# Paired routing counts, a first expert fed by columns, gathers in a row, and half tiles interleaved with whole ones

## The chip, the cores and the metric

The kernel runs on one core of a Trainium2 chip. The metric is the device time of one execution in microseconds (us); of several runs the median is taken. The engines are PE (TensorE, the matmuls), DVE (VectorE), ACT (ScalarE), POOL (GpSimd) and SP (SyncE, which here only issues DMAs). Below, a matmul written `128*64 128x256` holds a stationary operand of 128 rows by 64 columns in the array and streams 256 columns through it.

## The reference

Three layers follow each other: windowed attention over 3072 tokens (4 batches x 768), a mixture of experts with one expert for each token and a hard capacity of 384, and a second mixture with the two best experts of each token.

```python
def _moe_ref(x, w_gate, w1, w2):            # N=3072, D=512, E=8, F=1024
    cap = N // E
    order = np.argsort(-(x @ w_gate).flatten())
    for idx in order:                        # best (token, expert) pair first
        tok, e = int(idx) // E, int(idx) % E
        if assigned[tok] >= 0 or counts[e] >= cap:
            continue
        assigned[tok] = e
        counts[e] += 1
    for e in range(E):
        h = np.maximum(x[assigned == e] @ w1[e], 0.0)
        out[assigned == e] = h @ w2[e]

def _moe2_ref(x, w_gate, w_noise, noise, w1, w2):
    noisy = x @ w_gate + np.log1p(np.exp(x @ w_noise)) * noise
    top2 = ...                               # two best experts and their softmax weights
    for e in range(E):
        for k in range(2):
            mask = top2[:, k] == e
            h = np.maximum(x[mask] @ w1[e], 0.0)
            out[mask] += top2_w[mask, k, None] * (h @ w2[e])
```

## The kernel before, in words

`attention` (to about 104 us) is written out by hand. From there a planner, `Pipe`, lays down the order of all engines while the program is built: every instruction passes through `Eng.call` (line 68, so nearly all rows of the trace carry L68), which adds an estimated cost to a clock for its engine. The main thread issues the big matmuls; after nearly each one `tick` lets the generators (routing, gathers, weight splits, gates) issue what is due by those clocks. PE runs in the order so written and waits where an operand is late. Where the planner foresees a wait, `until` fills it with matmuls on `ones`.

**Routing** (`route`). Experts close one after another (k = 0 to 7). For each, the threshold is found digit by digit. A digit is a chain: DVE writes `GE` (token column x candidate, is the value at least the candidate), PE counts it against the one-hot `OH` into `rps`, DVE compares the counts with the capacity (`flf` or `flt`), PE sums the flags with one matmul on `onesb`, DVE turns the digit into new candidates (`d`, `ci`). Plan FAST (k = 0 with 5 digits left, k = 1 with 7) counts one column of 24 at a time: 24 matmuls of 31 by 8. Plan THRIFTY (k = 2 to 6, 8 digits) counts 8 columns at a time: 3 matmuls of 120 by 64, a copy by ACT (`blk`), 8 matmuls of 15 by 8 that add the diagonal blocks.

**First mixture** (`moe1`). For expert k `gather1` fetches 3 x 128 rows by POOL's indirect DMA and turns them to `xT`: by PE (`tps`, then a copy by ACT) for k = 0 and 1, by a DMA transpose later. `mm1` computes 8 blocks `ft` of hidden units, 12 matmuls of 384 columns each. A weight quarter w1[j] serves ft = 2j and 2j+1; it is loaded (`st`), normed (`junk`, `tot`), split by ACT into `w_h` and by DVE or POOL into `w_l`. Experts 0 to 4 do the second product in float32 (`m2f`), the others with split weights (`mm2`).

**Second mixture** (`moe2`). Expert e has two units: tiles 0, 1, 2 and a half tile (column 3, `HALF`), then tiles 4, 5, 6; experts 6 and 7 have no half tile. For each, `list2` builds the row list (with a small matmul `dup` for the half tile), `gathers2` gathers and transposes by DMA, `metas` reads what goes with the rows. `mm2` for a whole tile is 24 matmuls of 512 columns; for a half tile each of the 24 steps is cut into 2 matmuls `128*64 128x256` (e = 0, 1, 2) or 4 matmuls `128*32 128x128` (e = 3, 4, 5) that stand side by side in the array.

Of the kernel before, what the change touches and what calls it, by code (L numbers as in the profile page):

```python
# [8 lines left out]
F32 = mybir.dt.float32  # L9
# [63 lines left out]
class Pipe:  # L73
# [8 lines left out]

    def __init__(self, nc):
        self.t = {k: 0.0 for k in "pvsgyd"}
        self.ready = {}
        self.due = 0.0
        self.held = []
        self.early = set()
        self.gens = []
        self.V = Eng(nc.vector, self, "v")  # L90
        self.S = Eng(nc.scalar, self, "s")
        self.G = Eng(nc.gpsimd, self, "g")
        self.P = Eng(nc.tensor, self, "p")
        self.D = Eng(nc.sync, self, "y")

    def account(self, e, op, args, kw):
# [20 lines left out]
        if e == "p":  # L117
            if op == "transpose":
                n = aps[1].shape[0]
            else:  # L120
                n = size[0]
            cost = max(25.0, n * (4.0 if aps[1].dtype == F32 else 1.0) / 2.4 + 3.0)
        elif e == "v":
            rate = 0.52 if op in ("tensor_scalar", "tensor_copy") and not ps else 6.25 if op == "reciprocal" else 1.04
            cost = 69.0 + 60.0 * ptr + rate * n
        elif e == "s":
            cost = (51.0 if ps else 93.0) + 94.0 * (ptr or "accum_out" in kw) + 0.833 * n
        else:
            cost = 147.0 + 1.887 * n if op == "tensor_tensor" else (245.0 if ptr else 122.0) + 0.832 * n
# [474 lines left out]
class Plan:  # L604


    def __init__(self, name, bits, cols):
        self.name, self.cols = name, cols
# [7 lines left out]
FAST = Plan("f", (4, 3, 5, 5, 5, 5, 5), 1)  # L616
THRIFTY = Plan("t", (4,) * 8, 8)
NJ, NT, NH = 31, 15, 127


def route_setup(ctx, pool):
    memset = ctx.nc.gpsimd.memset
    ctx.capB = pool.tile([128, E], F32, name="capB")
    ctx.A = pool.tile([128, G], F16, name="assigned")
    ctx.bT = pool.tile([128, G], F32, name="bT")
    ctx.idx1 = pool.tile([128, E, CAP // 128], I32, name="idx1")
    ctx.est = pool.tile([1, E], I32, name="est")
    ctx.perm = pool.tile([1, E], I32, name="perm")
    ctx.left = pool.tile([NH, E], F32, name="left")
    ctx.flh = pool.tile([NH, E], BF16, name="flh")  # L630
# [4 lines left out]
    for plan in (FAST, THRIFTY):  # L635
        fl = pool.tile([max(plan.nj), len(plan.nj), E], BF16, name="fl" + plan.name)
        memset(fl, 0.0)
        setattr(ctx, "fl" + plan.name, fl)
    return [
        lambda: memset(ctx.capB, float(CAP)),  # L640
        lambda: memset(ctx.A, 0.0),
        lambda: memset(ctx.bT, 0.0),
    ]
# [120 lines left out]
def route(ctx):  # L764
# [36 lines left out]
    for k in range(E):  # L801
# [26 lines left out]
        plan = FAST if k < 2 else THRIFTY  # L828
        jtab = getattr(ctx, "jtab" + plan.name)
        off, NS = plan.off, len(plan.nj)  # L830
        FL = getattr(ctx, "fl" + plan.name)
        score = tl([128, E], F32, "score")
        R = tl([128, FAST.off[-1] + 1], I32, "R")[:, : off[-1] + 1]
# [34 lines left out]
        for s in range(s0, NS):  # L868
            nj, o = plan.nj[s], off[s]
            GE = tl([128, G * NJ], F16, "GE")[:, : G * nj].rearrange("p (c j) -> p c j", j=nj)  # L870
            step = G if k else G // 2
            for c in range(0, G, step):
                bc = [128, step, nj]
                V_.tensor_tensor(
                    GE[:, c : c + step], V[:, c : c + step].unsqueeze(2).to_broadcast(bc),
                    cand[:, :nj].unsqueeze(1).to_broadcast(bc), op=ALU.is_ge,
                )
# [14 lines left out]
            g = plan.cols  # L892
            cross = pst([g * nj, E, g])
            for c in range(0, G, g):
                P_.matmul(
                    cross.rearrange("p e c -> p (e c)"), GE[:, c : c + g].rearrange("p c j -> p (c j)"), OH[:, :, c : c + g],
                    start=(c == 0), stop=(c == G - g),
                )
# [7 lines left out]
            cnt = cross[:, :, 0]  # L906
            if g > 1:
                pipe.due = pipe.rdy("s", cross) + 900
                yield pipe.rdy("s", cross) - 200
                blk = tl([NT * THRIFTY.cols, E, THRIFTY.cols], F16, "blk")  # L910
                pipe.S.activation(blk, cross, AF.Copy)
                pipe.due = pipe.rdy("p", blk) + 450
                yield pipe.rdy("p", blk)
                cnt = pst([nj, E])
                for i in range(g):
                    P_.matmul(
                        cnt, ctx.id16[: g * nj, nj * i : nj * i + nj], blk[:, :, i], start=(i == 0), stop=(i == g - 1)
                    )
            pipe.due = pipe.rdy("v", cnt)
            yield pipe.due - 200  # L920
            fl = FL[:nj, s]
            V_.tensor_tensor(fl, cnt, capB[:nj], op=ALU.is_ge)
# [23 lines left out]
            else:  # L946
# [3 lines left out]
                ci = tl([128, NJ], I32, "ci")  # L950
# [94 lines left out]
def constants():  # L1045
# [10 lines left out]
    for plan in (FAST, THRIFTY):  # L1056
        jtab = [np.arange(1, n + 1) << sh for n, sh in zip(plan.nj[1:], plan.shifts[1:])] + [np.zeros(1)]
        f["jtab" + plan.name] = np.tile(np.concatenate(jtab).astype(np.int32), (128, 1))
# [18 lines left out]
KF = 5  # L1077
SLACKG = -200.0
# [3 lines left out]
SLACKH = 500.0  # L1082

# [59 lines left out]
def split(ctx, i, st, eager):  # L1143
# [59 lines left out]
    def halves(j, s):  # L1203
# [6 lines left out]
        sj = s[:, j : j + 1]  # L1210
        yield max(pipe.t["s"] - 100, pipe.rdy("s", s))
# [7 lines left out]
        a = 0  # L1219
        while a < 1024:  # L1220
# [8 lines left out]
            a = b  # L1229
        kn = KT if m == 0 else 2  # L1230
# [5 lines left out]
    for j in range(4):  # L1236
        if i == 0 and j > 1:
            yield lambda: 0 in ctx.X1
# [33 lines left out]
def mm1(ctx, k, xT, n, ps, last=True):  # L1272

    pipe, W, hT = ctx.pipe, ctx.W[k], []
    for ft in range(FT):
        if ft:

            pipe.until(lambda: len(hT) > ft - 3)
            ps = tile1(ctx)
        if ft % 2 == 0:  # L1280
# [3 lines left out]
        ps = ps[:, :n]  # L1284
        fs = slice(128 * (ft % 2), 128 * (ft % 2) + 128)
        i = 0
        for kt in range(KT):
            for wo, xo in ((0, 0), (0, 1), (1, 0)):
                pipe.P.matmul(
                    ps, w1[wo][:, kt, fs], xT[:, KT * xo + kt, :n], start=(i == 0), stop=(i == 3 * KT - 1)  # L1290
                )
                i += 1
                if i < 3 * KT:
                    pipe.tick()
        h = ctx.hp.tile([128, 2, XN], F16, tag="hT", name="hT", bufs=FT + 1)
# [45 lines left out]

def mm2_f32(ctx, k, hT):
# [18 lines left out]
def transpose(ctx, xT, rows, tile_):  # L1361

    pipe = ctx.pipe
    yield pipe.rdy("p", tile_)
    ps = ctx.m2.tile([128, 2 * KT, 128], F16, tag="m2", name="tps")
# [5 lines left out]
def gather1(ctx, k):  # L1371
# [3 lines left out]
    xT = ctx.xp.tile([128, 2 * KT, XN], F16, tag="xT", name=f"xT{k}", bufs=3)  # L1375
    ix = ctx.wk.tile([128, NA], F32, tag="ix1", name=f"ix1_{k}")
# [15 lines left out]
    for a in range(NA):  # L1392
        rows = xg[a][:, :DM].bitcast(F16)
        if k > 1:
            yield pipe.rdy("y", xg[a])
            pipe.D.dma_start_transpose(xT[:, :, 128 * a : 128 * a + 128], rows)
        else:
            yield from transpose(ctx, xT[:, :, 128 * a : 128 * a + 128], rows, xg[a])
# [120 lines left out]
def moe1(ctx):  # L1519
# [39 lines left out]
    for k in range(E):  # L1559
        ps = tile1(ctx)  # L1560
        if not k:
            pipe.until(lambda: 0 in ctx.gathered)
        pipe.until(lambda: k in ctx.X1 and k in ctx.W, ps)
        xT, ix = ctx.X1[k]
        hT = mm1(ctx, k, xT, CAP, ps)
# [16 lines left out]
def list2(ctx, e, pi, wt, cols, late=0.0):  # L1582
# [12 lines left out]
    if HALF in cols:  # L1595
# [3 lines left out]
        yield pipe.rdy("p", sh)  # L1599
# [120 lines left out]
def metas(ctx, e, u, cols, xg, meta):  # L1720
# [4 lines left out]
    yield pipe.rdy("v", *xg) + METAS * min(1.0, 0.5 * u)  # L1725
# [43 lines left out]
def moe2(ctx):  # L1769
    pipe = ctx.pipe  # L1770
    for e in range(E):
        k = E + e
        for h, cols in enumerate(units(e)):
# [8 lines left out]
            pv = ctx.pv.pop(u, None)  # L1782
            for c, a in enumerate(cols):
                ps = mm2(ctx, k, hT, 128 * c, parts(e) if a == HALF else 1, a == NA2 - 1)
# [133 lines left out]
def program(tc, t):  # L1918
# [3 lines left out]
    with (  # L1922
# [6 lines left out]
        with tc.manual_schedule(), tc.tile_pool(name="rt", bufs=1) as ctx.rt:  # L1929
            setup(ctx, cp)  # L1930
            attention(ctx)
            with (
# [14 lines left out]
                ctx.st, ctx.split, ctx.W, ctx.wfree = {}, {}, {}, [0.0] * 12  # L1947
                ctx.X1, ctx.Y, ctx.rowed, ctx.picked, ctx.gated = {}, {}, set(), 0, 0
# [3 lines left out]
                ctx.w2_read = ctx.wnext = 0  # L1952
# [149 lines left out]
```

## Time and profile before

| what | us |
|---|---|
| median of 3 runs | 1027.73 (1024.75 to 1029.03) |
| the profiled execution | 1033.36 |
| its span, first to last instruction | 1031.5 |
| PE busy | 982.5 (95%) |
| DVE busy | 639.0 (62%) |
| ACT busy | 466.7 (45%) |
| POOL busy | 284.4 (28%) |

The profiled execution is 5.6 us above the median. A row of the trace has its start and its length in us from the span's start; PE's lengths overlap, since the end of a matmul lies behind the start of the next one, so what a matmul costs PE is the distance from its start to the next start.

### The profile page before, as it was taken

The numbers are of one execution on the slowest core, as the hardware profiler recorded it, in microseconds if no ns is written. First come the engines' busy times: TensorE is split into PE (matmuls) and PEld (weight loads), VectorE is DVE, ScalarE is ACT, GpSimd is POOL, SyncE is SP. The second block draws the span as 40 slices with busy tenths as digits, with TensorE's granted clock in tenths as the row PEclk, the third lists the DMA queues.
The fourth block names the chain that finished last, engine by engine and source line by source line (L and its number), as shares of the span: only waits on it lengthen the run. The fifth ranks groups of instructions, "written<-read, shape, count | busy, mean of one in ns | idle before, by whom it ended". The sixth has DMA issues, their size and how long they took to land. (4 is left out here: it accounts for less than half of the span.)

```text
span 1031.5 us, 21798 instructions
## 1 busy us (share of the span) xinstructions
PE 982.5 (95%) x8278; PEld 589.7 (57%) x8278; DVE 639.0 (62%) x2095; ACT 466.7 (45%) x799; POOL 284.4 (28%) x468
## 2 busy tenths in 40 slices
PE   8989399999999999999989899999999999999997
PEld 5778377676767674554454454555544555555553
DVE  7988875676586776886757745457355454654221
ACT  6767153545262557977136445054260441523110
POOL 4765051010120312030223133133332332232221
PEclk9999599999999999999999999999999999999999
DMA  9998345575776759596188739367284591554410
GB/s 333 330 324 305 112 173 185 125 220 170 217 201 216 137 177 303 169 241 126 48 239 249 183 93 300 72 182 205 76 265 107 142 264 59 170 121 103 122 62 31
DMA packets 146848, 184.61 MB, mean 179 GB/s; under 512 B 105154, under 2 KB 105666, under 8 KB 145204
## 3 DMA queue, kind: packets, MB, share of 16 engines
q1 hardware_dynamic: 129410, 131.73, 44.7%
q0 software_dynamic: 13872, 45.15, 15.1%
q10 hardware_dynamic: 3458, 6.30, 1.7%
q8 instruction: 66, 1.08, 0.4%
q14 instruction: 42, 0.34, 0.1%
HBM read 127.10 MB, written 32.44 MB: 155 GB/s over the span
## 5 line engine op out<-in xcount | busy, mean ns | idle before, releaser
L68 PEld LDWEIGHTS <-hT 128*128 128x128 f16 (+2 forms) x1800 | 143.4, 98 | 163.3 <-issue 7.8
L68 ACT ACTIVATE hT<-m 128x384 f16<-128x384 f32 (+2 forms) x152 | 75.4, 499 | 282.2 <-PE m L68 258.3
L68 DVE SCALAR_TENSOR_TENSOR hT<-m,hT 128x384 f16<-128x384 f32 (+2 forms) x152 | 86.5, 570 | 105.6 <-ACT hT L68 91.2
L68 ACT ACTIVATE junk<-st 128x1024 f16<-128x1024 f32 x108 | 113.6, 1052 | 58.2 <-DMA st<-w_dram 30.2
L68 PE MATMUL m2f<-st,hT 128*128 128x256 f32 x480 | 127.6, 398 | 0.3 <-ACT hT L68 0.3
L68 POOL DMA_INDIRECT out_dram<-pv,ts x47 | 49.6, 1055 | 262.7 <-DVE pv L68 101.9
L68 DVE SCALAR_TENSOR_TENSOR pv<-m,ys,pv 128x512 f32<-128x512 f32 (+2 forms) x47 | 33.5, 714 | 117.4 <-PE m L68 117.3
L68 PE MATMUL m<-xT,w_0h 128*128 128x384 f16 (+2 forms) x384 | 97.9, 335 | 4.7 <-DMA xT<-xg 4.7
L68 PE MATMUL m<-xT,w_2h 128*128 128x384 f16 (+2 forms) x384 | 97.2, 333 | 1.7 <-DVE hT L68 1.7
L68 PE MATMUL m<-xT,w_3h 128*128 128x384 f16 (+2 forms) x384 | 97.1, 333 | 1.0 <-DVE hT L68 1.0
L68 PE MATMUL m<-xT,w_1h 128*128 128x384 f16 (+2 forms) x384 | 96.5, 331 | 0.0
L68 PEld LDWEIGHTS m2f<-st,hT 128*128 128x128 f32 x480 | 83.3, 190 | 10.0 <-ACT hT L68 0.7
L68 PE MATMUL m<-w_3h,hT 128*128 128x512 f16 (+2 forms) x300 | 71.7, 345 | 1.4 <-DVE hT L68 1.4
L68 PE MATMUL m<-w_2h,hT 128*128 128x512 f16 (+2 forms) x300 | 72.0, 345 | 0.9 <-issue 0.9
L68 PE MATMUL m<-w_0h,hT 128*128 128x512 f16 (+2 forms) x300 | 72.1, 346 | 0.0
L68 PE MATMUL m<-w_1h,hT 128*128 128x512 f16 (+2 forms) x300 | 71.5, 345 | 0.0
L68 PE MATMUL m<-xT,w_0l 128*128 128x384 f16 (+2 forms) x192 | 64.2, 335 | 0.0
L68 PE MATMUL m<-xT,w_2l 128*128 128x384 f16 (+2 forms) x192 | 64.0, 333 | 0.0
L68 PE MATMUL m<-xT,w_3l 128*128 128x384 f16 (+2 forms) x192 | 63.8, 332 | 0.0
L68 PE MATMUL m<-xT,w_1l 128*128 128x384 f16 (+2 forms) x192 | 63.5, 331 | 0.0
L68 POOL DMA_INDIRECT xg<-x,rows x54 | 54.2, 1004 | 29.5 <-issue 14.5
L68 POOL DMA_INDIRECT pv<-out_dram,tg x47 | 46.0, 979 | 51.7 <-DMA out_dram<-pv,ts 35.0
(350 smaller groups left out, 1827.4 us busy)
## 6 DMA issues: line engine op xcount, KB each, us to landing
st<-w_dram SPq DMA_DIRECT2D x64, 512.0 KB
st<-x_dram SPq DMA_DIRECT2D x64, 512.0 KB
v<-vctx_dram SPq DMA_DIRECT2D x24, 520.0 KB
k<-kT_dram SPq DMA_DIRECT2D x24, 312.0 KB
xr<-rb SPq DMA_DIRECT2D x24, 264.0 KB
x<-rb SPq DMA_DIRECT2D x24, 264.0 KB
q<-qT_dram SPq DMA_DIRECT2D x12, 512.0 KB
out_dram<-zero ACTq DMA_DIRECT2D x24, 256.0 KB
```

The lines of the kernel that those rows point to most:

```text
L68: return f(*args, **kw)
```

## The change

1. One plan of 7 digits (4, 3, 5, 5, 5, 5, 5 bits) serves all experts. Columns are counted in pairs: 12 matmuls of 64 by 16. The even column's counts stand in rows 0 to 31, the odd one's in rows 32 to 63, so the compare becomes two DVE instructions (`need`, then `fl`). ACT's `blk` copies are gone. For k > 1 a digit is not begun while a weight split is under way (`hungry`).
2. `first` computes ft = 0 and 1 of expert 0 for each 128-token column block as soon as it is transposed: 3 x 24 matmuls of 128 columns in the place of 24 of 384. The norms of weight quarters 2 and 3 no longer wait for `xT0`.
3. The transposes of expert 1 are issued 3 us later by the planner's clock, `dup` 1.5 us later.
4. The three gathers of the second unit (e = 0, tiles 4, 5, 6) are issued in a row; tile 6 is transposed by PE, 1.5 us after its planned landing, in a bank of `mm1`.
5. `mm2_both` computes the half tile and the whole tile ahead of it together: from the whole tile's 9th step on, one or two half-tile steps stand behind each whole-tile step.
6. The planner adds 50 to 150 ns where PE goes from one kind of matmul to another (`TURN`). The first unit's `metas` come 8 us later.

```diff
+    TURN = (0.0, 50.0, 150.0, 100.0)
...
+            kind = 2 if aps[1].dtype == F32 else int(n >= 256)
+            if kind != self.kind:
+                cost += self.TURN[kind + self.kind]
+                self.kind = kind
...
-FAST = Plan("f", (4, 3, 5, 5, 5, 5, 5), 1)
-THRIFTY = Plan("t", (4,) * 8, 8)
+PLAN = Plan((4, 3, 5, 5, 5, 5, 5))
+NT, NH, PAIR = 15, 127, 32
...
+            if k > 1 and ctx.hungry:
+                pipe.due = 0.0
+                yield lambda: not ctx.hungry
...
-            g = plan.cols
-            cross = pst([g * nj, E, g])
-            for c in range(0, G, g):
+            cross = pst([2 * PAIR, E, 2])
+            flat = cross.rearrange("p e c -> p (e c)")
+            for c in range(0, G, 2):
...
-            if g > 1:
...
-                blk = tl([NT * THRIFTY.cols, E, THRIFTY.cols], F16, "blk")
-                pipe.S.activation(blk, cross, AF.Copy)
...
-            V_.tensor_tensor(fl, cnt, capB[:nj], op=ALU.is_ge)
+            V_.scalar_tensor_tensor(need, cross[odd, :, 1], -1.0, capB[odd], op0=ALU.mult, op1=ALU.add)
+            V_.tensor_tensor(fl, cross[:nj, :, 0], need, op=ALU.is_ge)
...
+def first(ctx, tiles, spare):
...
+    for a in range(CAP // 128):
+        pipe.until(lambda: len(ctx.part0) > a and ctx.part0[a][1] <= pipe.t["p"] + 60.0, spare)
+        pipe.wait(*w1, spare=spare)
+        xT = ctx.part0[a][0]
+        for ft, ps in enumerate(tiles):
+            i = 0
+            for kt in range(KT):
+                for wo, xo in ((0, 0), (0, 1), (1, 0)):
+                    pipe.P.matmul(
+                        ps[:, 128 * a : 128 * a + 128], w1[wo][:, kt, 128 * ft : 128 * ft + 128], xT[:, KT * xo + kt],
+                        start=(i == 0), stop=(i == 3 * KT - 1),
+                    )
...
+BEHIND = 8
+def mm2_both(ctx, k, hT, s0, s1, cut):
...
+    for i, (ft, ho, wo) in enumerate(steps):
+        w2 = W["w2"][ft // 2]
+        pipe.P.matmul(
+            whole_, hT[ft][:, ho, s0 : s0 + 128], w2[wo][:, ft % 2], start=(i == 0), stop=(i == len(steps) - 1)
+        )
+        pipe.tick()
+        while done * (len(steps) - BEHIND) < (i + 1 - BEHIND) * len(steps):
+            ft, ho, wo = steps[done]
+            w2 = W["w2"][ft // 2]
+            for j in range(cut):
+                pipe.P.matmul(
+                    split_[m * j : m * j + m], hT[ft][:, ho, s1 : s1 + m], w2[wo][:, ft % 2, n * j : n * j + n],
...
+            done += 1
...
-        yield pipe.rdy("p", sh)
+        yield pipe.rdy("p", sh) + FAR1
...
-                yield max(pipe.rdy("g", rows), pipe.t["g"] - 100)
+                yield max(pipe.rdy("g", rows), pipe.t["g"] - 100 if u != 1 else 0.0)
...
+                if u == 1 and a == cols[-1]:
+                    yield from transpose(ctx, xT[:, :, s0 : s0 + m], g[:m, :DM].bitcast(F16), g, FAR1, "m1")
+                    continue
...
-                ps = mm2(ctx, k, hT, 128 * c, parts(e) if a == HALF else 1, a == NA2 - 1)
+                if HALF in cols and c == HALF - 1:
+                    both = mm2_both(ctx, k, hT, 128 * c, 128 * HALF, parts(e))
+                ps = both[a - HALF + 1] if both else mm2(ctx, k, hT, 128 * c, 1, a == NA2 - 1)
```

PE before, at the end of the first unit's whole tile 2 (`m2_8602`) and the start of its half tile (`m2_8636`):

```order
L68 MATMUL m2_8602<-w17_3h_8233,hT_8453 128x512
L68 LDWEIGHTS hT_8453
L68 MATMUL m2_8602<-w17_3l_8234,hT_8453 128x512
L68 LDWEIGHTS hT_8265
L68 MATMUL m2_8636<-w17_0h_8156,hT_8265 64x256
```

PE in the changed kernel, from the ninth step of the same whole tile (`m2_8343`), with the half tile (`m2_8344`):

```order
L68 MATMUL m2_8343<-w17_1l_7873,hT_8054 128x512
L68 LDWEIGHTS hT_8008
L68 MATMUL m2_8344<-w17_0h_7841,hT_8008 64x256
...
L68 LDWEIGHTS hT_8070
L68 MATMUL m2_8343<-w17_1h_7872,hT_8070 128x512
...
L68 MATMUL m2_8344<-w17_0l_7842,hT_8008 64x256
```

The half tile stood in one block behind the whole tile; now it stands in 16 groups of one or two steps, each between two matmuls that fill the array.

PE before, where the first big matmuls of expert 0 (`m1_2538`) begin and the flags of expert 1's first digit (`flf`) are summed:

```order
L68 MATMUL rps_1_3063<-OH_1_2978,GE_1_2986 31x8
...
L68 MATMUL m1_2538<-ones16_67 128x128
...
L68 MATMUL m1_2538<-xT0_2874,w0_0h_2925 128x384
...
L68 MATMUL rps_1_3113<-flf_95,onesb_69 128x8
```

PE in the changed kernel, at the same place:

```order
L68 MATMUL tps_2996<-id16_216,xg0_2_2835 128x128
...
L68 MATMUL rps_1_3013<-OH_1_2927,GE_97 64x16
L68 LDWEIGHTS w0_0h_2872
L68 MATMUL m1_2848<-xT0_2818,w0_0h_2872 128x128
L68 LDWEIGHTS onesb_69
L68 MATMUL rps_1_3041<-fl_95,onesb_69 128x8
L68 LDWEIGHTS w0_0l_2873
L68 MATMUL m1_2848<-xT0_2818,w0_0l_2873 128x128
```

Between the count of a digit and the sum of its flags stood 12 fillers and 3 matmuls of 384 columns; now one matmul of 128 columns stands there.

POOL before, at the second unit's gathers (`xg2_0_4` to `_6`), with the scatters of finished tiles (`z0`, `z1`):

```order
L68 DMA out_dram<-z0_8516,ts2_0_8045 3072x512
L68 DMA xg2_0_4_8586<-x2_61,rows2_0_8566 128x528
L68 DMA xg2_0_5_8593<-x2_61,rows2_0_8566 128x528
L68 DMA out_dram<-z1_8597,ts2_0_8045 3072x512
L68 DMA xg2_0_6_8606<-x2_61,rows2_0_8566 128x528
```

POOL in the changed kernel:

```order
L68 DMA out_dram<-z0_8255,ts2_0_7706 3072x512
L68 DMA xg2_0_4_8324<-x2_61,rows2_0_8304 128x528
L68 DMA xg2_0_5_8326<-x2_61,rows2_0_8304 128x528
L68 DMA xg2_0_6_8328<-x2_61,rows2_0_8304 128x528
L68 DMA out_dram<-z1_8338,ts2_0_7706 3072x512
```

The third gather went past the scatter of tile 1.

## Rows read from the trace of the kernel before

**Rows 1.** Waits of PE: who waited for whom; total us, times, longest.

```profile
PE m L68 <- DMA xT<-xg: 4.7, 1, 4.7
PE m L68 <- DVE hT L68: 4.1, 3, 1.7
PE dup L68 <- DVE lsh L68: 3.4, 4, 2.1
...
PE tps L68 <- DMA xg<-xr,idx: 1.5, 2, 1.1
```

**Rows 2.** Timeline, PE, one digit of expert 0: start, length, work, [idle before].

```profile
113.77 0.95 PE L68 MATMUL rps<-OH,GE 128*31 128x8 f16 x24 [1.06 <-DVE GE L68]
```

**Rows 3.** Timeline, PE, where expert 0's big matmuls begin and reach weight quarter 1's.

```profile
137.82 0.49 PE L68 MATMUL m<-xT,w_0h 128*128 128x384 f16 x2
...
143.02 0.49 PE L68 MATMUL m<-xT,w_1h 128*128 128x384 f16 x2
...
143.83 0.33 PE L68 MATMUL m<-xT,w_1l 128*128 128x384 f16 x1
144.09 0.80 PE L68 MATMUL rps<-OH,GE 128*31 128x8 f16 x24
144.82 0.50 PE L68 MATMUL m<-xT,w_1h 128*128 128x384 f16 x2
```

**Rows 4.** Timeline, DVE, ahead of the compare of expert 1's first digit.

```profile
136.72 1.14 DVE L68 TENSOR_TENSOR assigned<-assigned,T 128x24 f16<-128x24 f16 x1
137.79 0.15 DVE L68 TENSOR_TENSOR flf<-rps,capB 15x8 bf16<-15x8 f32 x1
```

**Rows 5.** Timeline, PE, one digit of expert 2 between big matmuls.

```profile
188.87 0.30 PE L68 MATMUL rps<-OH,GE 128*120 128x64 f16 x3
189.01 0.49 PE L68 MATMUL m<-xT,w_0h 128*128 128x384 f16 x2
...
189.75 0.37 PE L68 MATMUL rps<-blk,id 120*15 120x8 f16 x8
190.05 0.34 PE L68 MATMUL m<-xT,w_0h 128*128 128x384 f16 x1
...
190.65 0.17 PE L68 MATMUL rps<-flt,onesb 15*128 15x8 bf16 x1
190.75 0.34 PE L68 MATMUL m<-xT,w_0h 128*128 128x384 f16 x1
```

**Rows 6.** Timeline, PE, first half tile, then the second unit's start.

```profile
514.98 0.38 PE L68 MATMUL m<-w_3l,hT 128*128 128x512 f16 x1
515.29 0.41 PE L68 MATMUL m<-w_0h,hT 128*64 128x256 f16 x4
...
518.03 1.35 PE L68 MATMUL m<-ones 128*128 128x128 f16 x21
524.04 0.49 PE L68 MATMUL m<-xT,w_0h 128*128 128x384 f16 x2 [4.66 <-DMA xT<-xg]
```

**Rows 7.** Timeline, PE, half tiles of experts 3 and 4 (cut in four).

```profile
732.02 0.30 PE L68 MATMUL m<-w_0h,hT 128*32 128x128 f16 x8
...
733.73 0.50 PE L68 MATMUL m<-xT,w_0h 128*128 128x384 f16 x2
...
798.81 0.29 PE L68 MATMUL m<-w_0h,hT 128*32 128x128 f16 x8
...
801.32 0.50 PE L68 MATMUL m<-xT,w_0h 128*128 128x384 f16 x2
```

**Rows 8.** Table by stretch: length; busy us of PE, PEld, DVE, ACT, POOL; granted clock, DMA.

```profile
391.00:395.00 4.00, 4.00 (x17) 1.96 (x15) 2.65 (x5) 0.90 (x3) 2.54 (x6) 0.57 0.93 296
524.00:528.00 4.00, 3.96 (x15) 2.00 (x16) 0.44 (x5) 1.45 (x3) 1.01 (x1) 0.57 0.93 305
```

**Rows 9.** Timeline, POOL, a scatter, then the second unit's third gather.

```profile
512.20 1.02 POOL L68 DMA_INDIRECT out_dram<-z,ts  x1 [0.87 <-DVE z L68]
513.53 0.97 POOL L68 DMA_INDIRECT xg<-x,rows  x1 [0.30 <-issue]
```

More of the change, by code (lines that the diff above doesn't have):

```diff
@@ L634, in route_setup @@
     memset(ctx.left, float(CAP))
[L635 to L638, printed above, removed]
+    ctx.fl = pool.tile([max(PLAN.nj), len(PLAN.nj), E], BF16, name="fl")
+    memset(ctx.fl, 0.0)
+    ctx.GE = pool.tile([128, G, PAIR], F16, name="GE")
     return [
+        lambda: memset(ctx.GE, 0.0),
         lambda: memset(ctx.capB, float(CAP)),
@@ L1077 @@
 KF = 5
+FAR1 = 1500.0
 SLACKG = -200.0
@@ L1269, in tile1, with mm1 @@
     return ctx.m1.tile([128, DM], F32, tag="m1", name="m1")
-def mm1(ctx, k, xT, n, ps, last=True):
+def first(ctx, tiles, spare):
+    pipe, W = ctx.pipe, ctx.W[0]
+    pipe.until(lambda: len(W["w1"]) > 0, spare)
+    w1 = W["w1"][0]
+    for a in range(CAP // 128):
[10 more added lines that the diff above has]
+                    )
+                    i += 1
+                    if i < 3 * KT:
+                        pipe.tick()
+def mm1(ctx, k, xT, n, ps, last=True, done=()):
     pipe, W, hT = ctx.pipe, ctx.W[k], []
     for ft in range(FT):
-        if ft:
+        if ft and (ft != len(done) or not done):
             pipe.until(lambda: len(hT) > ft - 3)
-            ps = tile1(ctx)
-        if ft % 2 == 0:
+            ps = done[ft] if ft < len(done) else tile1(ctx)
+        elif done:
+            ps = done[ft] if ft < len(done) else ps
+        if ft % 2 == 0 and ft >= len(done):
             pipe.until(lambda: len(W["w1"]) > ft // 2, ps)
@@ L1283, in mm1 @@
             pipe.wait(*w1, xT, spare=ps)
-        ps = ps[:, :n]
         fs = slice(128 * (ft % 2), 128 * (ft % 2) + 128)
-        i = 0
-        for kt in range(KT):
+        i = 3 * KT if ft < len(done) else 0
+        out, spare = ps[:, :n], ps
+        if len(xT.shape) == 4:
+            out = out.rearrange("p (a n) -> p a n", n=128)
+        for kt in range(KT if not i else 0):
             for wo, xo in ((0, 0), (0, 1), (1, 0)):
+                x = xT[:, KT * xo + kt]
                 pipe.P.matmul(
-                    ps, w1[wo][:, kt, fs], xT[:, KT * xo + kt, :n], start=(i == 0), stop=(i == 3 * KT - 1)
+                    out, w1[wo][:, kt, fs], x if len(x.shape) == 3 else x[:, :n], start=(i == 0), stop=(i == 3 * KT - 1)
                 )
@@ L1339, in mm2 @@
     return ps
+def mm2_both(ctx, k, hT, s0, s1, cut):
+    pipe, W = ctx.pipe, ctx.W[k]
+    m, n = 128 // cut, DM // cut
+    steps = [(ft, ho, wo) for ft in range(FT) for ho, wo in ((0, 0), (1, 0), (0, 1))]
+    whole_, split_ = (ctx.m2.tile([128, w], F32, tag="m2", name="m2") for w in (DM, n))
+    done = 0
+    for i, (ft, ho, wo) in enumerate(steps):
[3 more added lines that the diff above has]
+        )
+        pipe.tick()
+        while done * (len(steps) - BEHIND) < (i + 1 - BEHIND) * len(steps):
[4 more added lines that the diff above has]
+                    split_[m * j : m * j + m], hT[ft][:, ho, s1 : s1 + m], w2[wo][:, ft % 2, n * j : n * j + n],
+                    start=(done == 0), stop=(done == len(steps) - 1),
+                )
+            done += 1
+    return whole_, split_
 def mm2_f32(ctx, k, hT):
@@ L1358, in mm2_f32, with transpose @@
     return ps
-def transpose(ctx, xT, rows, tile_):
+def transpose(ctx, xT, rows, tile_, late=0.0, bank="m2"):
     pipe = ctx.pipe
-    yield pipe.rdy("p", tile_)
-    ps = ctx.m2.tile([128, 2 * KT, 128], F16, tag="m2", name="tps")
+    yield pipe.rdy("p", tile_) + late
+    ps = getattr(ctx, bank).tile([128, 2 * KT, 128], F16, tag=bank, name="tps")
     for kt in range(2 * KT):
@@ L1559, in moe1 @@
     for k in range(E):
+        done = ()
+        if not k:
+            pipe.until(lambda: 0 in ctx.gathered and 0 in ctx.W)
+            done = tile1(ctx), tile1(ctx)
         ps = tile1(ctx)
-        if not k:
-            pipe.until(lambda: 0 in ctx.gathered)
+        if done:
+            first(ctx, done, ps)
         pipe.until(lambda: k in ctx.X1 and k in ctx.W, ps)
         xT, ix = ctx.X1[k]
-        hT = mm1(ctx, k, xT, CAP, ps)
+        hT = mm1(ctx, k, xT, CAP, ps, done=done)
         m1_done.add(k)
```

63 lines of the change are left out of this document (31 added, 32 removed).

## The prediction

> **What bounds the kernel now.** The page comes first: PE is busy 982.5 of 1031.5 us, so a change pays only by work that PE no longer does or by time in which PE no longer stands still. The waits of PE [rows 1] say which stands are left: one of 4.7 us for the gathered rows `xT`, 4.1 us in three waits for `hT`, 3.4 us in four waits of `dup`, 1.5 us for the rows that `tps` turns. The timeline of PE then shows what small work costs between big matmuls [rows 3, 5 to 7], and the table by stretch what a stand does to the clock [rows 8]. The working goes against the profiled execution, 1033.36 us; the median is 0.55% lower, and the same difference is then taken off it.
>
> Two prices recur. A matmul of 384 columns holds PE for 0.162 us: five lie between 143.02 and 143.83 [rows 3]; one of 512 columns by that 0.216. **A border** is the second: the matmul at 143.83 should give way at 143.99, the count starts at 144.09 [rows 3]. The half tile starts at 515.29, where the whole tile's last matmul, begun at 514.98, should have ended at 515.195 [rows 6]. So each time the array goes from the full 128 by 128 to a narrower shape PE loses about 0.095 us, and leaving the narrow shape costs the like.
>
> **Expert 0's digits.** A digit here is a chain with DVE ahead: PE waited 1.06 us for `GE` [rows 2]. Fewer count matmuls therefore give little. Behind the second half of `GE` stand 6 of them in place of 12 of 0.04 us (24 in 0.95 [rows 2]); if each takes half as long again, 0.11 us goes. The second compare instruction adds a dependent step of DVE: one compare is 0.15 us [rows 4], and with the handover I take 0.19. Five digits: 5 x (0.19 - 0.11) = **+0.4**.
>
> **First tiles by columns.** Before, the big matmuls begin at 137.82 and those of quarter 1 at 143.02 [rows 3]. In the new order one matmul of 128 columns stands between the first count of expert 1 and the sum of its flags. The flags come from DVE, whose `assigned` ran from 136.72 for 1.14 us with the compare only behind it at 137.79 [rows 4]. PE thus begins sooner, at about 136.9, and then stands until about 138.5. After that 70 matmuls remain, at 0.055 us each (a third of 0.162) 3.9 us, with a count, two flag sums and their borders: the end falls at 143.0 to 143.6, where it was 143.02. I take **+0.3**; without the wait it would be -1.7, and if the stand halves the clock for 4 us as elsewhere [rows 8], +2.
>
> **Counts of expert 1 and later ones.** A count of expert 1 costs a border and 144.82 - 144.09 = 0.73, together 0.825 [rows 3]. Twelve matmuls `64x16` are not in the trace. Nearest are the `31x8`, (0.73 - 0.095) / 24 = 0.027 us each; the other end is `120x64`, 3 in 189.01 - 188.87 = 0.14, 0.046 each and without a border [rows 5]. By the near end a count costs 12 x 0.027 + 0.19 = 0.51, and six digits of expert 1 give 6 x 0.32 = **-1.9**. A digit of experts 2 to 6 costs 0.14 + (0.30 + 0.095) + (0.10 + 0.10) = 0.735 [rows 5]; eight of them 5.9. The new one costs 0.51 + 0.20 = 0.71, seven of them 5.0. Five experts: **-4.6**. At the far end 41 counts would cost 12 x 0.019 x 41 = 9.3 more. I take the near end, because 16 columns stand closer to 8 than to 64. `blk` leaves ACT, which does not bound.
>
> **Two moves by the planner's clock.** `tps` of expert 1, 3 us later, meets rows that have landed: the longer wait of 1.1 goes [rows 1], **-1.0**. `dup`, 1.5 us later, loses its three short waits whole and 1.5 of the 2.1 [rows 1]: **-2.8** (-3.4 if nothing is left). What queues behind `dup` on PE only gains, and the half tile's list has time.
>
> **The second unit.** PE ran out of work at 518.03, spent 1.35 us on fillers and stood 4.66 until 524.04 [rows 6]: 6.0 us. Behind it the clock was granted 0.57 for 4 us [rows 8], another 1.7. The third gather began at 513.53 behind a scatter of 1.02 us that itself waited [rows 9]; in a row it begins about 1.9 us sooner. Its transpose moves from the queue to PE, 8 matmuls of 0.055, 0.45 us, placed inside the pair, and the first weights of the next stage are issued behind two transposes in place of three. With the wait gone the stage gives -6.0 - 1.7 + 0.45.
>
> **Pairs.** The half tile had one entry and one exit; now it stands in 16 groups among the whole tile's steps, 32 borders in place of 2. At 0.095 each pair grows by 2.85 us, if the border is paid there as at counts: the nearest rows, all of them narrow work between full matmuls, say so [rows 3, 5 to 7]. Six pairs, 17.1. Against that, a half tile cut in four took 733.73 - 732.02 = 1.71 for expert 3 and 801.32 - 798.81 = 2.51 for expert 4 [rows 7], the latter with two pauses in which the instructions came late. With full matmuls between, those pauses should go: 0.8 for each of experts 4 and 5, and some 0.8 for rounder packing, -2.4. First unit +2.85, the other five pairs **+11.8**; the second unit with its pair: -6.0 - 1.7 + 0.45 + 2.85 = **-4.4**.
>
> A row has the narrow matmul start 0.095 us behind the end of the full one, both ways [rows 3, 6]. The Trainium skill, "TensorEngine Tiling (Array Packing)", Key Properties, says that a change of tiling mode drains TensorE, and the trace agrees. "TensorE: Matmul & The Clock Gate", Step-by-step: what each phase is for, has weight loads pulled ahead of running matmuls, which would take the border away; the rows at hand speak against it for changes of shape.
>
> **The stalls for `hT`** (4.1 in all [rows 1], 1.7 more by the clock after one of them [rows 8]) hang on when DVE is free. The change moves DVE's work around them by less routing and another compare; I leave them, with 3 us either way.
>
> **Sum.** +0.4 + 0.3 - 1.9 - 4.6 - 1.0 - 2.8 - 4.4 + 11.8 = -2.2, so 1031.2 for the profiled execution and a median of 1025.4. What can be told from no change is about 0.5%, 5.1 us.
>
> **The rivals.** *A: interleaving hides the borders.* The weights of the next full matmul load while two narrow ones stream for 0.11 us each, and 32 borders cost nothing. (This is what the pull-ahead rule of the Trainium skill's "TensorE: Matmul & The Clock Gate", named above, would bring.) The pairs then give -2.4 and the two borders each had, 6 x -0.19; from -2.2 the sum falls by 17.1 and 1.1 to -20.4: 1007. The price of the border elsewhere speaks against it; but those rows all hold single short insertions, and none a series of the same two shapes. Chance 0.17.
>
> *B: slower, by the `64x16` count.* If its price follows the streamed counts in two banks of rows as `120x64` does, 46 ns, each of 41 counts costs 0.23 more, +9.3. It decides from 43 ns: there -2.2 + 12 x 0.016 x 41 is past +5. It gives 1033.36 + 7.1, a median of 1034.8. For it speaks that the stationary operand has 64 columns, twice the old; against it that the full-array `128x128` filler at 1.35 / 21 = 0.064 us [rows 6] carries eight times the columns and is hardly dearer than that. Chance 0.10.
>
> *C: the second unit still waits.* The gather gains only 1.9 us of 6.0, and `tps` stands in PE's order ahead of the pair's last steps; if the rows land later than it, PE stands there with the clock behind it. At half of 7.7 left: +3.9, a median of 1029.3. The pair itself fills 2.85 of the wait. Chance 0.15.
>
> *D: `hT` waits go.* With less on DVE the 4.1 and the clock's 1.7 vanish: -5.8, a median of 1019.6. Chance 0.13.
>
> **How the numbers follow.** The forecast has the remaining 0.45, and its own spread is about 4 us: it is faster by over 5.1 in a quarter of its cases, slower in one of twenty-five. Faster: 0.17 (A) + 0.12 (D, most of it) + 0.11 = 0.40. Slower: 0.10 (B, nearly all) + 0.02 (C) + 0.01 = 0.13. Within: 0.47. The range leaves out a tenth below, within A's reach, and a tenth above: 1008 to 1034.
>
> **What would show it.** In the changed profile: a whole tile with its half tile in 8.0 + 2.85 = about 10.9 us rather than 8.0 for experts 0 to 2 (sum term right), or below 8.2 (A); the `64x16` counts at 0.027 or 0.046 us each (B); a stand of PE of some 1.6 us ahead of the first flag sum of expert 1; no waits of `dup` but 0.6; no stand at the second unit's first matmul, and a granted clock of 1.0 behind it (else C); the waits for `hT` at 4.1 or none (D). Wrong most of all is the forecast if the border is not a price of the shape but of something that a series of pairs avoids.

## The result, and the profile after

| | us |
|---|---|
| median before | 1027.73 (1024.75 to 1029.03) |
| median after | 1041.34 (1038.40 to 1041.98) |
| ratio | 1.0131, 95% interval 1.0108 to 1.0155 |
| profiled execution, before and after | 1033.36 and 1038.40 |
| PE busy, before and after | 982.5 and 991.2 |

The changed kernel is slower by 11 to 16 us; the forecast was 1025.4, in a range of 1008 to 1034. The profiled executions lie only 5.0 us apart: the one of before was 5.6 above its median, the one of after 2.9 below. That alone is a lesson, told below.

The waits of PE in the changed profile (who waited for whom; total us, times, longest), against [rows 1]:

```profile
PE rps L68 <- DVE GE L68: 7.4, 10, 1.7
...
PE m L68 <- DVE hT L68: 2.8, 2, 2.6
...
PE rps L68 <- DVE fl L68: 2.2, 5, 0.4
```

The wait for `xT` and those of `dup`, 8.1 us in [rows 1], are gone, as the change meant. PE waits less and is still later: it has more to do. The timeline of PE (start, length, work) shows where, for a whole tile and its half tile of expert 2, which is called a pair here:

```profile
656.78 0.39 PE L68 MATMUL m<-w_1h,hT 128*128 128x512 f16 x1
657.10 0.30 PE L68 MATMUL m<-w_0l,hT 128*64 128x256 f16 x2
657.33 0.39 PE L68 MATMUL m<-w_1h,hT 128*128 128x512 f16 x1
657.65 0.41 PE L68 MATMUL m<-w_0h,hT 128*64 128x256 f16 x4
657.99 0.39 PE L68 MATMUL m<-w_1l,hT 128*128 128x512 f16 x1
```

From one whole-tile step to the next with one half-tile step between it takes 657.33 - 656.78 = 0.55 us, with two 657.99 - 657.33 = 0.66. A whole step is 0.216, a half step (two matmuls side by side) 0.11 to 0.12: 0.21 to 0.22 of each group is border, time that PE loses on entering and leaving the narrow shape, against 0.19 for two of 0.095 in the prediction. Fifteen groups more than before make 3.2 us a pair.

The counts, from the same timeline (the count in these rows stands where [rows 3] had 24 matmuls `31x8`):

```profile
142.62 0.22 PE L68 MATMUL m<-xT,w_0l 128*128 128x128 f16 x1
142.77 0.55 PE L68 MATMUL rps<-OH,GE 128*64 128x16 f16 x12
143.25 0.28 PE L68 MATMUL m<-xT,w_0h 128*128 128x128 f16 x2
```

Twelve matmuls take 143.25 - 142.77 = 0.48 with the border behind them, and with the one ahead 0.57. In each of the 42 counts from expert 1's first on, the matmuls of this profile follow each other at 33.5 ns on average, between the two prices that the prediction had (27 and 46).

And the first tiles:

```profile
137.10 0.55 PE L68 MATMUL rps<-OH,GE 128*64 128x16 f16 x12 [0.51 <-DVE GE L68]
137.58 0.23 PE L68 MATMUL m<-xT,w_0h 128*128 128x128 f16 x1
138.68 0.17 PE L68 MATMUL rps<-fl,onesb 15*128 15x8 bf16 x1 [0.88 <-DVE s L68]
...
145.76 0.48 PE L68 MATMUL m<-xT,w_1h 128*128 128x384 f16 x2 [0.67 <-ACT hT L68]
```

PE stands 0.51 us for `GE` ahead of the count and 0.88 ahead of the flag sum, with one matmul of 128 columns between; the forecast had some 1.6 ahead of the flag sum alone. The table by stretch (length; busy us of PE, PEld, DVE, ACT, POOL; granted clock, DMA share, GB/s) shows the clock behind it, 0.52, nearly all at the lower of its two levels (1.2 of 2.4 GHz). It is the "+2" that the prediction kept as a bound:

```profile
138.80:142.30 3.50, 3.50 (x36) 3.50 (x36) 2.74 (x8) 1.07 (x1) 2.50 (x3) 0.52 0.93 356
142.30:146.00 3.70, 3.03 (x53) 2.72 (x51) 1.18 (x7) 1.45 (x3) 0.00 (x0) 1.00 0.11 42
```

Both blocks then end together, and the third waits 0.67 us for ACT to empty a bank. Weight quarter 1 begins at 145.76 where [rows 3] had 143.02.

How far the first mixture had come when it was nearly done, expert 5's second product, before and after:

```profile
397.78 0.59 PE L68 MATMUL m<-w_0h,hT 128*128 128x512 f16 x2
```

```profile
397.68 0.59 PE L68 MATMUL m<-w_0h,hT 128*128 128x512 f16 x2
```

Up to there the forecast's terms (+0.4 + 0.3 - 1.9 - 4.6 - 1.0) had the changed kernel 6.8 us ahead; it is 0.1 ahead.

### The profile page after: what moved, and what is told of

It is laid out like the page before. It is cut to its first block, busy times and chain, and to the rows that moved or that the text cites. A ratio compares the mean times of both kernels' runs of the same rounds, so it can differ in the third digit from the quotient of the medians.

```text
span 1036.6 us, 21460 instructions
## 1 busy us (share of the span) xinstructions
PE 991.2 (96%) x8128; PEld 587.5 (57%) x8128; DVE 649.4 (63%) x2118; ACT 460.2 (44%) x760; POOL 286.8 (28%) x466
## 3 DMA queue, kind: packets, MB, share of 16 engines
q8 instruction: 65, 1.06, 0.4%
## 5 line engine op out<-in xcount | busy, mean ns | idle before, releaser
L68 ACT ACTIVATE hT<-m 128x384 f16<-128x384 f32 (+2 forms) x152 | 75.6, 500 | 290.7 <-PE m L68 289.1
L68 PE MATMUL m2f<-st,hT 128*128 128x256 f32 x480 | 120.3, 392 | 1.1 <-ACT hT L68 1.1
L68 PE MATMUL m<-xT,w_0h 128*128 128x384 f16 (+3 forms) x416 | 98.6, 323 | 0.0
L68 PEld LDWEIGHTS m2f<-st,hT 128*128 128x128 f32 x480 | 85.8, 189 | 11.6 <-ACT hT L68 1.5
L68 PE MATMUL m<-w_2h,hT 128*128 128x512 f16 (+2 forms) x300 | 74.2, 347 | 0.0
L68 PE MATMUL m<-xT,w_0l 128*128 128x384 f16 (+3 forms) x208 | 66.6, 323 | 0.0
L68 POOL DMA_INDIRECT xg<-xr,idx x24 | 26.1, 1086 | 122.4 <-issue 46.2
```

What stands on the lines that cost most here:

```text
L68: return f(*args, **kw)
```

## The experiments

Theory 1: the pairs cost their borders, some 3 us each, and that is the loss; the waits that the forecast counted as savings were long in one execution only; the counts save PE little. Theory 2: the loss is in the routing, where DVE's wider compares hold up PE. The kernels below were timed in four sets on different chips, each beside runs of the kernel before on the same chip (medians 1024.5, 1024.8, 1024.5 and 1031.5 us); the ratios are to those, with their 95% intervals, and a difference in us is the ratio's.

**The kernel before once more** (`b_copy`, no edit).

> The kernel before, unchanged, for a second profile. Theory 1 (the profiled execution on which the forecast was summed, 1033.4 us, was one with a late gather and long dup waits, which the median of 1027.7 does not have): the stand of PE before the second unit's first matmul is well under 4.7 us or the dup waits under 3.4 us in all, and the span is near 1026. Theory 2 (these waits are there in every execution): the stand is again 4 to 5 us, the dup waits 3 to 3.5 us.

Its time was 1027.86. Waits of PE in this second profile of the same program:

```profile
PE m L68 <- DMA xT<-xg: 3.4, 1, 3.4
...
PE tps L68 <- DMA xg<-xr,idx: 2.8, 2, 2.2
...
PE dup L68 <- DVE lsh L68: 0.6, 2, 0.4
```

Against [rows 1]: 3.4 for 4.7, `dup` 0.6 for 3.4, `tps` 2.8 for 1.5. The waits for DMA are a matter of the execution, and the 2.1 us of `dup` is not there again. So it is theory 1, though the wait for `xT` is there in both.

A third thing differs. The pairs of experts 3, 4 and 5 took 18.70, 19.51 and 18.66 us in the profile of before and take 17.90, 18.00 and 17.70 in `b_copy`. In the first profile the half tiles cut in four pause 3 times, 1.06 us in all, for nothing that the trace shows. Such pauses stand in all four profiles of the fourth set (1.3 to 3.1 us), and in no other profile of this study with the half tile in a block.

**The interleaving alone, and all without it.** `b_both` is the kernel before with

```diff
-                ps = mm2(ctx, k, hT, 128 * c, parts(e) if a == HALF else 1, a == NA2 - 1)
+                if HALF in cols and c == HALF - 1:
+                    both = mm2_both(ctx, k, hT, 128 * c, 128 * HALF, parts(e))
+                ps = both[a - HALF + 1] if both else mm2(ctx, k, hT, 128 * c, 1, a == NA2 - 1)
```

with `mm2_both` as in the changed kernel, and `a_sep` is the changed kernel with this edit turned back.

> The kernel before with the interleaving of half tile and whole tile alone. Theory 1 (32 borders of about 0.09 us for each of six pairs): each pair grows by 2.3 to 3.4 us at experts 0 to 2 and 1.5 to 2.4 at 3 to 5, in all +12 to +16 us, so 1040 to 1043. Theory 2 (the loss lies in the routing, by the dearer counts and DVE's wider compares; the pairs cost little): +3 at most, 1031 or less.

> The changed kernel with the half tile again as one block behind its whole tile, all else as changed. Theory 1: 1041.3 less 12 to 16, so 1025 to 1029, the time of before. Theory 2: 1038 or more.

`b_both`: 1039.5 us, ratio 1.0153 (1.0123 to 1.0183), +15.7 us. `a_sep`: 1022.09, ratio 0.9972 (0.9948 to 0.9996), -2.9. The interleaving is the whole loss; all other edits together are a small gain, where the forecast had -2.2 - 14.65 = -16.85. From the start of the second product to expert 2's next unit the profile of `a_sep` needs 19.19 us and that of after 22.60, 3.41 more; the other pairs of experts 1 and 3 to 5 are longer by 3.19 to 3.29. Six pairs by themselves would cost 19.7. In `b_both` the five later ones are 3.2 to 3.4 longer than in `b_copy`, 16.4 in all, while the first, which ends ahead of the wait for the second unit's rows, fills that wait: from its second product to the second unit 23.06 us for 23.97. The changed kernel, too, takes 2.1 us less than `a_sep` from there to expert 1's second product (50.20 for 52.34), where `a_sep` waits. In `a_sep` the block stands whole again (timeline of PE):

```profile
656.97 0.38 PE L68 MATMUL m<-w_3l,hT 128*128 128x512 f16 x1
657.28 0.41 PE L68 MATMUL m<-w_0h,hT 128*64 128x256 f16 x4
657.52 0.28 PE L68 MATMUL m<-w_0l,hT 128*64 128x256 f16 x2
657.63 0.39 PE L68 MATMUL m<-w_0h,hT 128*64 128x256 f16 x4
```

Three steps take 657.63 - 657.28 = 0.35 us, two of them inside the changed kernel's groups 0.24 and a border each way.

**Fewer groups** (`a_coarse`), the changed kernel with four groups of six half steps:

```diff
-        while done * (len(steps) - BEHIND) < (i + 1 - BEHIND) * len(steps):
+        while (i + 1 - BEHIND) % 4 == 0 and done * (len(steps) - BEHIND) < (i + 1 - BEHIND) * len(steps):
```

> The changed kernel with the half tile's 24 steps in 4 groups of 6 behind whole-tile steps, in place of 16 groups of one or two. Theory 1 (each group costs its two borders, 0.21 to 0.22 us together by the changed profile, whatever it holds): 12 groups fewer in each of six pairs, 72 x 0.215 = -15.5 against the changed kernel, so 1022 to 1027 beside a before of 1024 to 1028, and each pair longer than block and whole tile apart by about 0.65 us. Theory 2 (what costs is that the two accumulations run side by side, whatever the number of groups): 1038 or more.

1026.06 us, ratio 1.0021 (1.0003 to 1.004), where the changed kernel has 1.0131 and `a_sep` 0.9972: 11 us of the 16 are back. In the profiles its pairs of experts 1 to 5 are 0.66 to 0.69 us longer than in `a_sep`, which is three groups more at 0.22; that would have given 15.5 back, and the runs, of another set, show 4 less. The price is per group and not per step, and theory 2 falls. That PE goes to another accumulation and back is not what costs either. In the profile of before, a matmul on the full array that writes another tile (`tot`) stands between two steps of an open accumulation:

```profile
395.81 0.33 PE L68 MATMUL m<-xT,w_3h 128*128 128x384 f16 x1
395.97 0.17 PE L68 MATMUL tot<-sq,onesb 128*128 128x4 bf16 x1
396.00 0.32 PE L68 MATMUL m<-xT,w_3h 128*128 128x384 f16 x1
```

It holds PE for 0.03 us, its own short work, with no border. What costs is the change of shape; whether PE waits there for its array to empty or for the weights was not separated.

**The pair counts.** `b_pair` is the kernel before with the plan of seven digits, the matmuls `64x16` and `need`; `b_pair_hungry` holds a digit back during a split as well; `b_pair_hungry_metas` also reads the first unit's meta data later:

```diff
+            if k > 1 and ctx.hungry:
+                pipe.due = 0.0
+                yield lambda: not ctx.hungry
...
-    yield pipe.rdy("v", *xg) + METAS * min(1.0, 0.5 * u)
+    yield pipe.rdy("v", *xg) + METAS * (1.0 if u > 1 else 0.5)
```

> The kernel before with the counts in pairs of columns and seven digits for all experts alone (without the hold-back of digits during weight splits). My forecast had -6.1 us for it (+0.4, -1.9, -4.6). Theory 1 (the count costs 0.57 instead of 0.51 and DVE's chain is longer, so that the gain shrinks): -4 to +1. Theory 2 (the wider compares hold up DVE and, by it, PE in the first mixture): +5 or more.

> The kernel before with the pair counts and the hold-back of a digit while a weight split is under way. Theory 1 (the loss of the pair counts alone came from DVE's wider compares standing in front of weight splits, for which PE waited on fillers): the 91 fillers near 204 to 210 us go, and the time is 4 to 7 us below that of the pair counts alone, at 1023 to 1026 beside a before of 1024.5. Theory 2 (the dearer count itself is the loss): the time stays within 2 us of the pair counts alone.

> The kernel before with pair counts, hold-back and the first unit's meta data read 8 us later. Theory 1 (in the run without this, DVE stood 4.1 us for a gather before the meta data, the weight splits piled up behind it and PE stood 3.75 us for hT with the clock down after it): 3 to 6 us below pair counts with hold-back alone, 1020 to 1024 beside a before of 1024.5. Theory 2: no difference, 1027 or more.

1030.35 (1.0058, 1.0038 to 1.0079), 1028.97 (1.0043, 1.0028 to 1.0059) and 1024.16 (0.9997, 0.998 to 1.0013). So +6, +4.4 and 0 (-0.3), where the forecast had -6.1. `b_pair` shows theory 2's mechanism in small: while DVE does routing, the split of a weight quarter is late, and PE runs on fillers. PE in the first fence, DVE at the same place in the second:

```profile
203.76 0.84 PE L68 MATMUL m<-ones 128*128 128x128 f16 x12
204.50 0.94 PE L68 MATMUL m<-ones 128*128 128x128 f16 x14
205.48 1.96 PE L68 MATMUL m<-ones 128*128 128x128 f16 x32
...
207.85 1.07 PE L68 MATMUL m<-ones 128*128 128x128 f16 x16
208.95 1.12 PE L68 MATMUL m<-ones 128*128 128x128 f16 x17
```

```profile
208.59 0.73 DVE L68 SCALAR_TENSOR_TENSOR w_3l<-st,s,w_3h 128x512 f16<-128x512 f32 x1
...
209.66 0.94 DVE L68 TENSOR_TENSOR GE<-V,ci 128x744 f16<-128x744 f32 x1
```

Those 91 fillers are gone with the hold-back (between 150 and 300 us 25 fillers remain of 110). But of the 5 us that they took the time shows 1.5 only, the number of that run's theory 2, though by another way. In `b_pair_hungry` the routing ends at 347 us, in the kernel before at 369, and DVE comes to the meta data of the second mixture before the gather has landed; the weight splits pile up behind, and `hT` behind them. DVE there, then PE, then the table by stretch:

```profile
444.13 0.17 DVE L68 COPY meta<-xg 128x2 f32<-128x2 f32 x1 [4.11 <-DMA xg<-x,rows]
...
452.92 1.41 DVE L68 SCALAR_TENSOR_TENSOR w_3l<-st,s,w_3h 128x512 f16<-128x512 f32 x2
454.33 0.56 DVE L68 SCALAR_TENSOR_TENSOR hT<-m,hT 128x384 f16<-128x384 f32 x1
```

```profile
454.94 0.80 PE L68 MATMUL m<-xT,w_1h 128*128 128x384 f16 x2 [3.75 <-DVE hT L68]
```

```profile
455.00:459.00 4.00, 4.00 (x13) 1.81 (x13) 1.70 (x6) 2.87 (x9) 0.35 (x3) 0.50 0.91 236
```

A stand of 3.75 us, and the clock at half in the 4 us behind it. With the meta data read later, 4.7 us come back, as theory 1 expected.

**The moves alone** (`b_gathfar`: gathers in a row, third tile by PE, later meta data, later `tps` and `dup`; `b_far`: the last two alone), and **the first tiles alone** (`b_first`).

```diff
-                yield max(pipe.rdy("g", rows), pipe.t["g"] - 100)
+                yield max(pipe.rdy("g", rows), pipe.t["g"] - 100 if u != 1 else 0.0)
...
-        yield pipe.rdy("p", sh)
+        yield pipe.rdy("p", sh) + FAR1
```

> The kernel before with the gathers of the second unit in a row, its third tile turned by PE, the later reading of the first unit's meta data, and the later issue of the second expert's transposes and of dup: none of the counts, the first tiles or the pairs. The forecast gave these -1.0 - 2.8 and for the second unit's wait and clock -7.25, in all -11. Theory 1 (the waits were shorter in ordinary executions than in the one profiled): -5 to -8 against before. Theory 2 (the forecast's prices hold): -11. Theory 3 (tps in the stage waits itself): -2 to 0.

> The kernel before with the later transposes of expert 1 and the later dup alone. The forecast gave them -3.8. Theory 1 (their waits are shorter in most executions): -1 to -3. Theory 2: -4 or more. The rest of the -5.2 that these and the gathers in a row gave together is then the gathers'.

> The kernel before with the first two hidden blocks of expert 0 computed by token columns alone. Theory 1 (PE stands for the flags of expert 1 with one matmul in front, the clock falls behind it, and both blocks end together so that the third waits for its bank): +1 to +4. Theory 2 (the earlier start pays): -1 to -2.

`b_gathfar` 1020.47 (0.9949, 0.9927 to 0.997), -5.2 us; `b_far` 1029.76 (0.9984, 0.9969 to 0.9999), -1.6; `b_first` 1026.09 (1.0022, 0.9998 to 1.0045), +2.3 with an interval that reaches zero. `b_gathfar` has the lowest ratio of this study, though its interval overlaps that of `a_sep`. It and its repeat below have `tps` waiting 1.2 and 0.9 us for the rows, rival C in small.

**All but pairs and first tiles** (`a_sep_nofirst`, and `b_pair_gathfar` without the planner's turn costs).

> The changed kernel without the interleaved pairs and without the first tiles by columns: pair counts with hold-back, gathers in a row, later meta data, transposes and dup, the planner's turn costs. Theory 1 (the pair counts do save some 8 us in the first mixture, as the profile of pair counts with hold-back shows, and alone they lost it again at waits that the other moves remove; the first tiles cost 1 to 3): 1013 to 1018 beside a before of 1024.5. Theory 2 (the pair counts lose in themselves, and the moves give -5 whatever they stand with): 1020 or more.

> The same without the planner's turn costs (50 to 150 ns where PE changes its kind of matmul). Theory 1 gives the same 1013 to 1018; a difference of over 3 us to its twin would be the turn costs' own, by a better or worse order of the work.

1021.59 (0.9972, 0.9951 to 0.9992) and 1023.48 (0.999, 0.9967 to 1.0013). Theory 1's 1013 to 1018 fell: with the moves the pair counts bring nothing that can be told, and both ratios are above that of `b_gathfar` (other chips, intervals that overlap). The first tiles show no cost in the time when the rest stands with them (`a_sep` has the same ratio as `a_sep_nofirst`), nor do the turn costs. Yet the profile of `b_pair_gathfar` (its shortest execution, 1017.3) was 5 us shorter than that of `b_gathfar` in the first mixture. Repeated profiles say where it goes.

> A second profile of pair counts, hold-back, gathers in a row and later transposes, dup and meta data; the first profile came from the shortest of its twelve executions (1017.3, median 1023.5). Theory 1 (the routing gain of some 5 us is in every execution, and longer ones lose it at PE's waits for DVE and DMA further on): the stretch from expert 0's first big matmul to expert 5's second product is again 252 to 256 us, and the waits after it are 3 us or more longer than in the first profile. Theory 2 (the gain itself varies): that stretch is 258 us or more.

> A third profile of the same kernel. The same two theories: 252 to 256 us from expert 0's first big matmul to expert 5's second product and longer waits behind it, or 258 us and more in that stretch itself.

> A second profile of the moves without the pair counts, as the measure for the two above: the stretch from expert 0's first big matmul to expert 5's second product at 257 to 260 us (258.3 in the first profile) by both theories.

From expert 0's first big matmul to expert 5's second product: 258.3 and 258.2 us without pair counts, 252.9, 253.0 and 252.9 with them. The gain of 5.3 us is there each time, to a tenth. But the stretch begins later: expert 0's first big matmul lies 28.8 and 28.6 us behind the first count without pair counts, and 31.4, 31.6 and 31.6 with them. From the first count to expert 5's second product it is 287.1 and 286.8 us against 284.2, 284.6 and 284.6, so 2.5 us remain. `a_sep_nofirst`, which has the turn costs besides, takes 287.2; `a_sep`, with the first tiles too, 289.2; the changed kernel 289.1; before 288.9. So by one profile each the turn costs take back the 2.5 us and the first tiles lose another 2. Behind that stretch the second and third profile of the pair counts (1030.07 and 1028.66 us) wait for gathered rows, PE in each:

```profile
554.70 0.90 PE L68 MATMUL m<-xT,w_0h 128*128 128x448 f16 x2 [4.54 <-DMA xT<-xg]
...
627.50 0.54 PE L68 MATMUL m<-xT,w_0h 128*128 128x448 f16 x2 [2.58 <-DMA xT<-xg]
```

```profile
620.20 0.90 PE L68 MATMUL m<-xT,w_0h 128*128 128x448 f16 x2 [3.96 <-DMA xT<-xg]
```

The table by stretch of the first of them:

```profile
550.00:554.00 4.00, 0.16 (x1) 0.00 (x0) 3.30 (x5) 1.00 (x1) 0.00 (x0) 1.00 1.11 287
554.70:558.00 3.30, 3.30 (x10) 1.36 (x10) 0.00 (x0) 0.00 (x0) 0.98 (x1) 0.55 1.02 405
```

The DMA engines are busy throughout, PE stands, and the clock is at half behind it. `b_gathfar_2` (1023.54) has one wait for `xT` in all, of 0.44 us. PE comes 2.5 us sooner to rows that do not come sooner. What limits those rows was not tried, but the DMA queue of SP shows a candidate for the first of them, in `b_gathfar_2` and then in the second profile of the pair counts:

```profile
534.63 7.79 SPq L68 DMA_TRANSPOSE xT<-xg  x4
```

```profile
535.71 7.32 SPq L68 DMA_TRANSPOSE xT<-xg  x3
543.89 2.13 SPq L68 DMA_DIRECT2D st<-x_dram  x4
546.12 2.10 SPq L68 DMA_TRANSPOSE xT<-xg  x1
```

With the pair counts the planner puts the unit's fourth transpose behind four weight loads, in all three profiles.

## Why the prediction was wrong, step by step

The forecast was a small gain and the result a loss of 13.6 us. By the runs, the pairs cost what was forecast, nearly (15.7 for 14.65), and all else brought -2.9 for -16.85. The step that failed is that second sum: the gain of the counts (-6.1 forecast, between +6 and 0 measured) and the waits that were to go (-11 forecast, -5.2 measured).

**The translation from profile to median.** The forecast summed -2.2 us against an execution of 1033.36 and took 0.55% off the result. Against the profile of after it missed by 1038.4 - 1031.2 = 7.2 us; of the 7.2, 6.7 lie ahead of expert 5's second product (0.1 for 6.8). The remaining 8.7 of the 15.9 came from this step: 5.8 were taken off, and the profile of after lay 2.9 below its own median. Waits that the change removes were part of what made the execution of before long, so they cannot be saved and taken off again. The two profiles of before show it: `dup` 3.4 and 0.6. Priced by `b_copy` the same terms have 1.3 less on the second unit's stand, 2.2 less on `dup`, no 2.4 for pauses and 1.1 more on `tps`: -2.2 + 1.3 + 2.2 + 2.4 - 1.1 = +2.6, a median of 1030.3 without any other insight.

**Pairs**: the mechanism held, the size was short. Sum of the step: 2.85 + 11.8 = 14.65 forecast, 15.7 measured alone and about 16 in the changed kernel. That the sums lie so close is partly luck: each border is 0.105 rather than 0.095, so a pair grows by 3.2 to 3.4 instead of 2.85, 19.7 in all, and what the first pair cost went into a wait. The -2.4 for pauses in the half tiles of experts 3 to 5 was again a feature of executions: those three pairs took 0.8 to 1.5 us less each in `b_copy` than in the profile of before, with no edit, and against `a_sep` they grew by as much as the others.

**Counts**: "-1.9" and "-4.6" are the terms that failed most. The price of a count was 0.57 and not 0.51 (33.5 ns a matmul), 41 x 0.06 = 2.5 us less to gain; rival B's point of decision, 43 ns, was not reached. Of the rest, 2.5 us arrive at expert 5's second product where the counts stand with the moves. There the failure is to have booked them at the end of the program: with PE sooner, the meta data's gather, then the rows of later units were late, and the clock fell after some of the stands. What is late next was asked of the second unit, but not of time taken out of PE's own work. In the changed kernel even the 2.5 us are not there: the planner's turn costs, for which the forecast had no term, and the first tiles lie against them, by one profile each.

**Expert 0's digits**: +0.2 a digit forecast as +0.08. Before, the first and the fifth of these counts begin at 108.92 and 118.62, a period of 2.43 us; now it is 112.66 - 110.03 = 2.63:

```profile
110.03 0.18 PE L68 MATMUL rps<-fl,onesb 31*128 31x8 bf16 x1 [0.44 <-DVE fl L68]
111.28 0.95 PE L68 MATMUL rps<-OH,GE 128*64 128x16 f16 x12 [1.07 <-DVE GE L68]
112.66 0.18 PE L68 MATMUL rps<-fl,onesb 31*128 31x8 bf16 x1 [0.44 <-DVE fl L68]
```

The dependent step costs 0.2 as forecast; half as many matmuls save nothing of the chain.

**First tiles**: a stand was forecast; the lower clock was kept as a bound and came in the changed profile, but in the profiles of `a_sep` and `b_first`, with the same first tiles, 138.8 to 146 us was granted 1.00. The wait of 0.67 for the bank was overlooked. Alone +2.3 (0 to +4.6); with the rest the time shows nothing, one profile each +2.

**Moves**: `tps` and `dup` -1.6 for -3.8 forecast; with the second unit -5.2 for -11. In the changed kernel the stand at the second unit's start went, as forecast (no rival C). The direction was right, the size was that of one long execution.

**Rivals.** A is refuted by the pairs' own rows and by `a_coarse`: borders are not hidden in a series. In the words of the Trainium skill, "TensorEngine Tiling (Array Packing)", Key Properties, a change of tiling mode drains the engine; the 0.22 us per group of this trace agrees. The Trainium skill's "TensorE: Matmul & The Clock Gate", Step-by-step: what each phase is for, lets weight loads go ahead of running matmuls; the groups here, at 0.22 us of border each, show no such cover across a change of shape. D came in part: `hT` waits were 2.8 us in place of 4.1, and the lower clock behind one of them did not come. B's argument from the filler misreads [rows 6]: 0.064 us is a row's whole length over 21, while fillers in a row follow each other at 0.056. The slower side was given 0.13, for a mechanism that was not the one.

## What to carry to other kernels

Work that leaves part of the array idle should stand in one block: here every group of it between full matmuls paid two borders, 0.22 us, and the price was counted in groups, not in work. Time taken out of the bounding engine counts only as far as its operands come sooner too; ask which gather, split or bank is next before booking it. And before waits are priced as savings, see them in a second execution: here two executions of the same program lay 5.5 us apart, and the stretches with the waits on which the sum rested (the pairs of experts 3 to 5, that of expert 1 with its `dup`, the second unit's start) differed by 6.2 us. And an edit that only moves the planner's clocks needs its own term in the sum, since it reorders everything behind it.

## What was not expected of the hardware

A matmul of 64 stationary columns that streams 16 takes 33.5 ns in a row of twelve, where one of 31 that streams 8 took 27 [rows 3]. Which of the two, the wider operand or the longer stream, makes the difference was not tried. And a stand of PE is not always followed by the lower clock: in the changed profile PE stood 2.56 us for `hT` in expert 5's first product, and the granted clock behind it was 1.00:

```profile
389.86 0.48 PE L68 MATMUL m<-xT,w_2h 128*128 128x384 f16 x2 [2.56 <-DVE hT L68]
```

```profile
390.00:394.00 4.00, 4.00 (x26) 2.43 (x25) 3.19 (x6) 3.63 (x9) 0.00 (x0) 1.00 0.95 299
```

Before, it stood a shorter time in the same product, and the clock behind it was 0.57 [rows 8], most of it at the lower level:

```profile
390.23 0.48 PE L68 MATMUL m<-xT,w_2h 128*128 128x384 f16 x2 [1.72 <-DVE hT L68]
```

Ahead of that stand PE had run 24 short matmuls (`slps`, 12 columns each), which in the changed kernel do not stand there. What decides between the two stays open.
